# Two-stage attention and top-1 experts: the split of W1 and the first slot's row division moved behind the attention loop, routing moved by three places

## The chip, the cores and the metric

The kernel runs on one core of a Trainium2 chip, as one launch. The metric is the device time of an execution in microseconds. Before the change three executions took 689.18, 688.70 and 688.98 us; their median is 688.98. The profile belongs to a further, profiled execution.

The core has a matrix engine (PE, with its weight loads shown apart as PEld), a vector engine (DVE), a scalar engine (ACT), a general engine (POOL) and a queue engine (SP) that starts DMAs. Each engine runs its own list of instructions in order; semaphores join them.

## The reference

Attention in two steps makes `x`, and a mixture of experts with one expert per row makes the output:

```python
p_packed = sm_attn(p, k, v)              # batch 8, heads 8, p: 32 rows, k and v: 576 rows, head_dim 64
out = sm_attn(q, p_packed, p_packed)     # q: 576 rows
x = out.transpose(0, 2, 1, 3).reshape(4608, 512)

logits = x @ w_gate + modality_bias[modality_id]     # 8 experts
e_idx = argmax(logits); gate_w = softmax(logits)[e_idx]
for e in range(8):                                   # w1: 8 x 512 x 1024, w2: 8 x 1024 x 512
    h = maximum(x[mask_e] @ w1[e], 0)
    out[mask_e] = gate_w[mask_e] * (h @ w2[e])
```

## The kernel before

**Attention.** The work is cut into eight units: unit 2i+g holds the batches 2i and 2i+1 and half g of the heads. A unit goes through: loads of `k`, `v`, `q`; transposes on DVE (`kT`, `qT`, L224); first scores on PE (L234 with `kT`, `pT`); their negated maxima on DVE (`nb`, L246); exponentials on ACT (`a`, L251); transposes of these on PE (L272, L278) with copies on ACT; the packing matmuls (L289); division and sum on DVE (`bd` L294, `pc` L301); a transpose of the packed rows (L308, `ppT` L311); gate products (L321); second scores (L234 with `qT`, `ppT`); their maxima and subtraction on DVE (`m` L336, `mB` L340 and L343); exponentials on ACT (`a2T`, L348); the output matmuls (L357) in three parts; and ACT's copies of each part to `xs` (L364, the unnormalised rows, stored to `x_scr` in HBM) and to `lt` (L366, gate logits and row sums).

**The order.** The units are pipelined. A table written by hand, `ORDER`, names the steps of one period; each has a number of `>` that says how many units ahead it belongs. Inside this loop the order on PE, DVE, ACT and SP is as written; POOL, and everything behind the loop, is ordered by a scheduler. An entry `e` of the table pulls one piece, up to the next `yield`, out of a list `todo`. That list first holds constants and then gets `route(i)` once both units of pair i have finished their output matmuls.

**Routing.** `route(i)` runs `routing(i)` for the 1152 rows of pair i: logits, the arg maximum and a scan on DVE (L400 to L425, ending in `inc`), prefix sums on PE (L431 to L433, which wait for `inc`), places and gate weights (L436 to L452, `dsi` and `meta`), and nine scatters of row numbers by POOL (L455). Pair 0 adds the choice of the first expert. Pair 1 adds: the load of that expert's W1 (L631), table a of the slots, the fetches of the lists and rows of slots 0 and 1 by POOL (`pre`: L647, L650), the split of W1, and the row division of slot 0. Pair 2 adds table b. Pair 3 is routed behind the loop, together with table c.

**The split.** `split_w` makes of a weight a rounded high part on ACT (`w1h`, `w2h`, L642) and the remainder on DVE (`w1l`, `w2l`, L643), each in four parts of 128x1024. `st_n` divides a slot's gathered rows by their sums on DVE (`rx` L664 and L665, `xn` L666), once for each half of 128 rows.

**Slots.** Behind the loop 19 slots of up to 256 rows each follow. A slot: transposes of `xn` (PE L673), high and low part (`x_hl`, ACT L675, DVE L676), W1 products (PE L686: high by high, high by low, low by high), ReLU in two parts (ACT L690, DVE L691), W2 products (PE L723), scaling (ACT L727) and a scatter of output rows by POOL (L728). Rows of the slot after next are gathered meanwhile (L647, L650). Weights are split again, under an `If`, only where the expert changes. The first `If` (L834, in `sw(0, 0)`) is about W1 of the first slot, whose W1 is already split; it isn't taken.

Of the kernel before, what the change touches and what calls it, by code (L numbers as in the profile page):

```python
# [23 lines left out]
def packed_attn_moe_kernel(  # L24
# [75 lines left out]
    def routing_consts(pool):  # L100
        for z in range(0, PAD, P):
            nc.sync.dma_start(lst.rearrange("(e r) w -> r e w", e=E)[z:z + P], pad)
        mid4 = pool.tile([P, NP, NC, 2], I32, name="mid4")
        bias2 = sm.tile([P, 2, E], F32, name="bias2", bufs=1)
        nc.sync.dma_start(bias2, mod_bias[None].broadcast_to([P, 2, E]))
        nc.sync.dma_start(mid4.rearrange("p i c w -> p i (c w)"),
                          mod_id.bitcast(I32).rearrange("(i p m) -> p i m", p=P, m=2 * NC))
        for w in range(2):
            nc.gpsimd.iota(meta.rearrange("p (i c) w -> p i c w", c=NC)[:, :, :, w], pattern=[[P * NC, NP], [1, NC]],
                           base=0, channel_multiplier=NC)  # L110
        nc.gpsimd.tensor_copy(out=m1, in_=mid4[:, :, :, 0])
        m1v = m1.rearrange("p i c -> p (i c)")[:, :, None]
        nc.gpsimd.tensor_scalar(out=m0, in0=m1v, scalar1=-1.0, scalar2=1.0, op0=ALU.mult, op1=ALU.add)
        bias_t = pool.tile([P, NT, E], F32, name="bias_t")
        nc.gpsimd.tensor_tensor(out=bias_all, in0=m0.broadcast_to([P, NT, E]),
                                in1=bias2[:, 0:1, :].broadcast_to([P, NT, E]), op=ALU.mult)
        nc.gpsimd.tensor_tensor(out=bias_t, in0=m1v.broadcast_to([P, NT, E]),
                                in1=bias2[:, 1:2, :].broadcast_to([P, NT, E]), op=ALU.mult)
        nc.gpsimd.tensor_tensor(out=bias_all, in0=bias_all, in1=bias_t, op=ALU.add)
# [11 lines left out]
    xts = [cw.tile([P, 2, 2, GW], F32, name=f"xt{n}") for n in range(2)]  # L131
# [8 lines left out]
    W = dict(raw1=cw.tile([P, KD * F], F32, name="raw1"))  # L140
# [41 lines left out]
    def load_p(q, i0, i1):  # L182
        q.dma_start(pz[:, 4 * i0:4 * i1], p.rearrange("b (g h) j d -> (h j) (b g) d", h=HG)[:, 4 * i0:4 * i1])
# [335 lines left out]
    def first_expert():  # L519
        cnt, mxc = st_("cnt"), st_("mxc", 1)  # L520
        tt(out=cnt, in0=base[1], in1=base0, op=ALU.subtract)
        nc.vector.tensor_reduce(mxc, cnt, axis=AX.X, op=ALU.max)
        nc.vector.scalar_tensor_tensor(out=cnt, in0=cnt, scalar=mxc, in1=desc[:, 0, :], op0=ALU.is_equal, op1=ALU.mult)
        e0 = const.tile([P, 1], F32, name="e0")
        nc.vector.tensor_reduce(e0, cnt, axis=AX.X, op=ALU.max)
        tsc(out=e0, in0=e0, scalar1=-1.0, scalar2=float(E), op0=ALU.mult, op1=ALU.add)
        e0i = const.tile([P, 1], I32, name="e0i")
        nc.vector.tensor_copy(out=e0i, in_=e0)
        return e0, e0i
# [87 lines left out]
    def val(tb, s, col, engines, lo, hi):  # L617
        return nc.values_load(tb[s:s + 1, col:col + 1], engines=engines, min_val=lo, max_val=hi,  # L618
                              skip_runtime_bounds_check_because="bounded by the routing")
# [5 lines left out]
    def load_w(w, which, e):  # L625
        src, n = ((w1, KD), (w2, KF))[which]
        m = src.shape[2]
        d = w["raw" + "12"[which]].rearrange("p (j f) -> p j f", j=n)
        sv = src[ds(e, 1)].rearrange("a (j p) f -> p (a j) f", p=P)
        for j in range(0, n, n // 2):  # L630
            ins = nc.sync.dma_start(d[:, j:j + n // 2], sv[:, j:j + n // 2])  # L631
        return ins_of(ins)

    def split_w(w, which, eng=None, zs=range(4)):
        hi, lo = w["12"[which] + "h"], w["12"[which] + "l"]
        n, m = hi.shape[1], hi.shape[2]
        r = w["raw" + "12"[which]].rearrange("p (j f) -> p j f", j=n)
        for z in zs:
            c = (slice(None), slice(z * n // 4, (z + 1) * n // 4), slice(None))
            if which == 0:  # L640
                c = (slice(None), slice(None), slice(z * m // 4, (z + 1) * m // 4))
            nc.scalar.copy(out=hi[c], in_=r[c])  # L642
            (eng or nc.vector).tensor_tensor(out=lo[c], in0=r[c], in1=hi[c].bitcast(F32), op=ALU.subtract)  # L643
# [16 lines left out]
    def st_n(xt, M):  # L660
        for t in range(2):
            xr = xt[:, t].rearrange("p g (r k) -> p (g r) k", r=4)
            rs = sm.tile([P, H, 1], F32, name="rx")
            nc.vector.tensor_scalar_add(rs, xr[:, :, D:XW], 1e-9)  # L664
            nc.vector.reciprocal(rs, rs)  # L665
            tt(out=M["xn", t].rearrange("p (h d) -> p h d", d=D), in0=xr[:, :, 0:D], in1=rs.broadcast_to([P, H, D]),  # L666
               op=ALU.mult)
# [74 lines left out]
    def pre(n):  # L742
        if n < NS_:
            fetch(*slot_of(n), mts[n % 4], xts[n % 2])

    E0 = []
    with ExitStack() as actx:
        A = dict(ld=actx.enter_context(tc.tile_pool(name="ld", bufs=1)), lp=actx.enter_context(tc.tile_pool(name="lp", bufs=1)),
                 ps=actx.enter_context(tc.tile_pool(name="ps", bufs=4, space=PSUM)))
        us = [attention(n // 2, n % 2, lts[n // 2], A) for n in range(NU)]  # L750

        def rest():
            routing_consts(A["lp"])
            yield

        def route(i):
            yield from routing(i, lts[i], A["ps"])
            if i == 0:
                E0.extend(first_expert())
                yield  # L760
            if i == NA[0] - 1:
                E0.append(val(E0[1], 0, 0, (ET.SP,), 0, E - 1))
                load_w(W, 0, E0[2])
                yield
                T.append((yield from table_phase("a", E0[0], NA[0], None, SA[0])))
                yield
                for n in range(2):
                    pre(n)
                for z in range(4):
                    split_w(W, 0, None, (z,))  # L770
                    yield
                st_n(xts[0], W)
                yield
            if i == NA[1] - 1:
                T.append((yield from table_phase("b", T[0]["last"], NA[1], T[0]["used"], SA[1] - SA[0])))

        todo, seen = [rest()], {}

        def more():
            while todo:  # L780
                try:
                    next(todo[0])
                    return
                except StopIteration:
                    todo.pop(0)

        def step(m, nm):
            next(us[m][nm])
            if m == 0 and nm == "dk":
                load_p(nc.scalar, 0, 2)  # L790
                load_p(nc.scalar, 2, NP)
            if nm == "k0" and m in (0, 1, 2, 3):
                prep_p(A["ps"], 2 * m, nc.scalar.copy if m else nc.vector.tensor_copy)
            seen[m, nm] = seen.get((m, nm), 0) + 1
            if nm[0] == "x" and m % 2 and m // 2 < NA[1] and all(seen.get((m, f"x{z}"), 0) == 3 for z in range(3)):
                todo.append(route(m // 2))

        with tc.manual_schedule(engines={ET.PE, ET.DVE, ET.Activation, ET.SP}):
            for n in range(-6, NU + 6):
                for z in ORDER.split():  # L800
                    nm = z.lstrip("<>")
                    m = n + z.count(">") - z.count("<")
                    if nm == "e":
                        if 0 <= m:
                            more()
                    elif 0 <= m < NU:
                        step(m, nm)
            while todo:
                more()
    wraw = ctx.enter_context(tc.tile_pool(name="wraw", reuse_waits="tile", bufs=1))  # L810
# [147 lines left out]
```

## Time and profile before

| what | value |
|---|---|
| median of three executions | 688.98 us (688.70 to 689.18) |
| the profiled execution | 689.62 us |
| its span, first to last instruction | 688.0 us |
| mean granted clock of PE in the span | 0.935 |
| PE busy | 585.0 us, 85% of the span |
| DVE busy | 296.8 us, 43% |
| ACT busy | 208.1 us, 30% |
| POOL busy | 195.1 us, 28% |

The shares are averages over two stages: some 213 us of attention, in which PE, DVE and ACT wait for each other, and the slots. In the rows below, a line such as `L643 DVE TENSOR_TENSOR w1l<-raw,w1h x3` means three instructions of line 643 on DVE that write `w1l` from `raw` and `w1h`; the bracket names the idle time of the engine ahead of them and what ended it. One execution of the split of W1 (four parts) lies in the loop; three more lie in the slots, at 337, 426 and 653 us.

### The profile page before, as it was taken

What the parts mean: (1) busy time and instruction counts of PE and PEld (TensorE: products, weight loads), DVE (VectorE), ACT (ScalarE), POOL (GpSimd) and SP (SyncE); (2) the same over time, 40 slices, a digit from 0 to 9 for tenths busy, and PEclk for the clock granted to TensorE, in tenths of its full rate; (3) what the DMA queues carried; (4) which work ended last, traced back from release to release, by engine and by line L of the source; (5) the groups of instructions that cost most, each with busy time, mean ns of one, the idle gap of its engine ahead of it and who ended that gap; (6) DMA issues with size and microseconds to landing.
All of it is one profiled execution on the core that took longest, in us unless ns stands there. A gap on an engine that the chain in (4) does not pass through costs nothing. (4 is left out here: it accounts for less than half of the span.)

```text
span 688.0 us, 13217 instructions
## 1 busy us (share of the span) xinstructions
PE 585.0 (85%) x5156; PEld 511.0 (74%) x5156; DVE 296.8 (43%) x701; ACT 208.1 (30%) x373; POOL 195.1 (28%) x226
## 2 busy tenths in 40 slices
PE   2687876765674889999999999899999999999990
PEld 1566654453553879898998898888998899889980
DVE  3375974877785632222451123712311231122290
ACT  1355532424334112121441125411221122122360
POOL 4000113043233633212312343412331233223340
PEclk9999988877776999999999999999999999999996
DMA  9464797770381544111196122631111111112121
GB/s 300 166 229 167 223 337 206 263 280 20 116 316 71 186 156 155 46 46 47 48 335 232 37 66 68 223 108 49 49 50 45 48 48 47 47 49 48 44 61 28
DMA packets 39053, 87.02 MB, mean 126 GB/s; under 512 B 11120, under 2 KB 11120, under 8 KB 37936
## 3 DMA queue, kind: packets, MB, share of 16 engines
q1 hardware_dynamic: 26560, 63.15, 25.9%
q0 software_dynamic: 9264, 22.13, 10.9%
q8 instruction: 52, 0.85, 0.5%
q10 hardware_dynamic: 3136, 0.56, 0.5%
q14 instruction: 41, 0.34, 0.2%
HBM read 66.42 MB, written 19.39 MB: 125 GB/s over the span
## 5 line engine op out<-in xcount | busy, mean ns | idle before, releaser
L686 PE MATMUL ps_h<-x_hl,w1h 128*128 128x256 f32 x1088 | 203.6, 286 | 2.1 <-ACT w1h L642 0.7
L686 PEld LDWEIGHTS ps_h<-x_hl,w1h 128*128 128x128 f32 x1088 | 171.9, 192 | 5.5 <-ACT w1h L642 1.1
L686 PE MATMUL ps_h<-x_hl,w1l 128*128 128x256 f32 x544 | 154.2, 283 | 4.5 <-DVE pref L590 2.4
L691 DVE SCALAR_TENSOR_TENSOR hl<-ps_h,hh 128x512 fp32r<-128x512 f32 x68 | 46.8, 691 | 216.2 <-ACT hh L690 191.7
L723 PE MATMUL ps_o<-w2h,hh 128*128 128x512 f32 x296 | 116.3, 393 | 0.8 <-ACTq L852 0.8
L723 PE MATMUL ps_o<-w2h,hl 128*128 128x512 f32 x296 | 116.1, 392 | 0.0
L723 PE MATMUL ps_o<-w2l,hh 128*128 128x512 f32 x296 | 115.9, 392 | 0.0
L650 POOL DMA_INDIRECT xt<-x_scr,mt x92 | 93.1, 1012 | 71.2 <-issue 24.2
L686 PEld LDWEIGHTS ps_h<-x_hl,w1l 128*128 128x128 f32 x544 | 104.3, 192 | 5.4 <-DVE pref L590 2.6
L690 ACT ACTIVATE hh<-ps_h 128x512 fp32r<-128x512 f32 x68 | 40.6, 599 | 173.8 <-PE ps_h L686 98.5
L728 POOL DMA_INDIRECT out_dram<-ot,mt x37 | 38.6, 1044 | 179.5 <-ACT ot L727 113.0
L727 ACT ACTIVATE ot<-ps_o,mt 128x512 f32<-128x512 f32 x37 | 25.5, 690 | 131.2 <-PE ps_o L723 105.9
L723 PEld LDWEIGHTS ps_o<-w2h,hl 128*128 128x128 f32 x296 | 55.8, 188 | 11.5
L723 PEld LDWEIGHTS ps_o<-w2h,hh 128*128 128x128 f32 x296 | 55.7, 188 | 11.5 <-ACTq L852 1.2
L357 PE MATMUL ps<-bd,a2T 128*128 128x146 f32 x288 | 53.6, 343 | 12.1 <-ACT a L251 5.7
L723 PEld LDWEIGHTS ps_o<-w2l,hh 128*128 128x128 f32 x296 | 55.7, 188 | 10.9
L357 PEld LDWEIGHTS ps<-bd,a2T 128*128 128x128 f32 x288 | 47.3, 232 | 20.9 <-ACT a L251 7.9
L455 POOL DMA_INDIRECT lst<-meta,dsi x36 | 34.9, 970 | 84.7 <-DVE meta L452 33.2
L647 POOL DMA_DIRECT2D mt<-lst x23 | 17.3, 752 | 72.1 <-DMA out_dram<-ot,mt 40.6
L673 PE MATMUL ps_t<-ident,xn 128*128 128x128 f32 x168 | 26.5, 284 | 10.3 <-ACT lt L366 6.1
L289 PE MATMUL ps<-ld_v,a1T 64*64 64x128 f32 x576 | 23.3, 313 | 11.3 <-ACT a1T L280 9.1
L664 DVE TENSOR_SCALAR rx<-xt 128x8 f32<-128x8 f32 x44 | 6.0, 171 | 59.9 <-DMA xt<-x_scr,mt 59.9
(190 smaller groups left out, 671.9 us busy)
## 6 DMA issues: line engine op xcount, KB each, us to landing
raw<-in_moe_w_dram SPq DMA_DIRECT2D x24, 1024.0 KB
x_scr<-xs SPq DMA_DIRECT2D x8, 1170.0 KB
raw<-in_k_dram SPq DMA_DIRECT2D x16, 576.0 KB
ld_v<-in_v_dram SPq DMA_DIRECT2D x16, 576.0 KB
raw<-in_q_dram SPq DMA_DIRECT2D x16, 576.0 KB
xt<-x_scr,mt POOLq DMA_INDIRECT x92
out_dram<-ot,mt POOLq DMA_INDIRECT x37
lst<-meta,dsi POOLq DMA_INDIRECT x36
```

Of the source, the lines that this page charges most:

```text
L289: nc.tensor.matmul(pp[64 * u:64 * u + 64, a, 0:P].rearrange("p (r d) -> p r d", r=2), a1T[rows, c, 64 * u:64 * u + 64], v_t[rows, 2 * u:2 ...
L357: nc.tensor.matmul(xp[:, a, 2 * c * XL:2 * c * XL + 2 * XL], a2T[:, 3 * z + c, a], bd[:, a].rearrange("p r k -> p (r k)"), start=True, sto ...
L455: ins = ins_of(nc.gpsimd.indirect_dma_start(out=lst, out_offset=bass.IndirectOffsetOnAxis(ap=dsi[:, c:c + 1], axis=0), in_=meta[:, i * NC ...
L647: ins = [nc.gpsimd.dma_start(mt, lst[ds(off, P2), :].rearrange("(t p) w -> p t w", p=P))]
L650: ins.append(nc.gpsimd.indirect_dma_start(out=xt[:, t, g], out_offset=None, in_=x_scr[g][0:NA[ph] * 2 * S] if ph < 2 else x_scr[g], in_off ...
L673: nc.tensor.transpose(out=ps[:, j], in_=M["xn", t][:, j * P:j * P + P], identity=ident)
L686: nc.tensor.matmul(ps[:, f], M[a][:, j, (f0 + f) * P:(f0 + f) * P + P], x[:, j, b], start=(m == 0), stop=(m == 3 * KD - 1))
L690: ia = nc.scalar.activation(out=M["hh"][:, fs], in_=ps, func=AF.Relu)
L691: iv = nc.vector.scalar_tensor_tensor(out=M["hl"][:, fs], in0=ps, scalar=0.0, in1=M["hh"][:, fs].bitcast(F32), op0=ALU.max, op1=ALU.subtract)
L723: nc.tensor.matmul(op, M[a][:, j, t * P:t * P + P], M[b][:, j, :], start=(n == 0), stop=(n == 3 * KF - 1))
L727: nc.scalar.activation(out=ot, in_=op, func=AF.Copy, scale=mt.bitcast(F32)[:, t, 2:3])
L728: nc.gpsimd.indirect_dma_start(out=out, out_offset=bass.IndirectOffsetOnAxis(ap=mt[:, t, 1:2], axis=0), in_=ot, in_offset=None, bounds_che ...
```

## The change

Two edits. Three bare `yield`s stand at the start of every `route(i)`: each piece of routing comes three `e` entries later. And the four parts of the split of W1, with the row division of slot 0, leave `route(1)`, where each was pulled by an `e`, and stand behind the loop's last step, ahead of what is left in `todo`.

```diff
         def route(i):
+            yield
+            yield
+            yield
             yield from routing(i, lts[i], A["ps"])
             if i == 0:
                 E0.extend(first_expert())
@@
                 yield
                 for n in range(2):
                     pre(n)
-                for z in range(4):
-                    split_w(W, 0, None, (z,))
-                    yield
-                st_n(xts[0], W)
-                yield
             if i == NA[1] - 1:
@@
                     elif 0 <= m < NU:
                         step(m, nm)
+            for z in range(4):
+                split_w(W, 0, None, (z,))
+            st_n(xts[0], W)
             while todo:
                 more()
```

On DVE, around the first maxima of unit 7 (`nb`) and the second maxima of unit 6 (`m`, `mB`), the list before is:

```order
L541 CAST tab_a<-tab_f 128x7
L643 TENSOR_TENSOR w1l<-raw_111,w1h 128x4x256 x3
L246 TENSOR_REDUCE nb<-ps 128x1 x2
L643 TENSOR_TENSOR w1l<-raw_111,w1h 128x4x256
L664 TENSOR_SCALAR rx<-xt_104 128x8
L665 RECIPROCAL rx<-rx 128x8
L666 TENSOR_TENSOR xn_106<-xt_104,rx 128x512
L664 TENSOR_SCALAR rx<-xt_104 128x8
L665 RECIPROCAL rx<-rx 128x8
L666 TENSOR_TENSOR xn_107<-xt_104,rx 128x512
L336 TENSOR_REDUCE m_1968<-ps 128x9 x2
L340 STREAM_TRANSPOSE mB<-m_1968 128x576
```

At the same place of DVE, the list now is:

```order
L541 CAST tab_a<-tab_f 128x7
L246 TENSOR_REDUCE nb<-ps 128x1 x2
L336 TENSOR_REDUCE m_1952<-ps 128x9 x2
L340 STREAM_TRANSPOSE mB<-m_1952 128x576
L336 TENSOR_REDUCE m_1957<-ps 128x9 x2
L343 TENSOR_TENSOR mB<-ps,mB 128x576
```

The split and the division are gone from between table a and the maxima of both units; ACT's casts of `w1h` are gone from around the exponentials of unit 7 in the same way.

On PE, between unit 7's gate products (L321) and its second scores (L234 with `qT`), the list before is:

```order
L321 MATMUL ps<-wg_132,ppT 32x16 x13
L834 UNCONDITIONAL_BRANCH
L840 UNCONDITIONAL_BRANCH
L321 MATMUL ps<-wg_132,ppT 32x16 x3
L431 LDWEIGHTS ones_b
L431 MATMUL ps<-inc,ones_b 128x72
L432 LDWEIGHTS negtri
L432 MATMUL ps<-oh,negtri 128x72
L433 LDWEIGHTS ones_b
L433 MATMUL ps<-inc,ones_b 128x8
L234 MATMUL ps<-qT,ppT 32x288 x32
```

At the same place of PE, the list now is:

```order
L321 MATMUL ps<-wg_132,ppT 32x16 x16
L234 MATMUL ps<-qT,ppT 32x288 x32
L357 MATMUL ps<-bd_114,a2T_126 128x146 x6
L431 LDWEIGHTS ones_b
L431 MATMUL ps<-inc,ones_b 128x72
L432 LDWEIGHTS negtri
L432 MATMUL ps<-oh,negtri 128x72
L433 LDWEIGHTS ones_b
L433 MATMUL ps<-inc,ones_b 128x8
L357 MATMUL ps<-bd_115,a2T_127 128x146 x18
```

The prefix sums of pair 2 stand behind the second scores and part of unit 6's output now. In the same way those of pairs 0 and 1 moved from ahead of the second scores of units 3 and 5 to behind their transposes; those of pair 3, which stood inside slot 0's W1 products, now stand ahead of slot 0. On DVE the chain L400 to L425 of pair 2 still stands ahead of unit 7's second maxima; the steps from L436 to L445, which stood ahead of them too, now follow them.

On DVE behind the loop, the list now has, after 35 rows of pair 3's routing and table b, two parts of `w2l` among eight short rows, and then:

```order
L541 CAST tab_b<-tab_f 128x7
L643 TENSOR_TENSOR w1l<-raw_111,w1h 128x4x256 x4
L664 TENSOR_SCALAR rx<-xt_104 128x8
L643 TENSOR_TENSOR w2l<-raw_2300,w2h 128x1024 x2
L443 CAST dsi<-dsf 128x9
L475 TENSOR_SCALAR tl_f<-rem 128x8
L497 TENSOR_SCALAR key<-eidx,last_b 128x8
L618 TENSOR_LOAD tab_a
L835 COMPARE_AND_BRANCH
```

Then come the first division of slot 0 (`xn_106`), the second (`xn_107`, nine rows later), and the low parts `x_hl`. So all four parts of `w1l` and of `w2l` now stand ahead of slot 0's rows on DVE; before, `xn` and `w1l` were made in the loop, and the four parts of `w2l` stood behind slot 0's `x_hl`. On ACT the four casts of `w1h`, and then those of `w2h`, stand ahead of slot 0's `x_hl`. On POOL the gathers of slots 2 and 3 stood ahead of pair 3's nine scatters, and stand behind them now. On SP the load of the first W1 stands behind one load of `v` that it preceded.

## The prediction

> **What bounds the kernel now.** I read the slices and the chain of work that ended last first, then the table of windows, then the rows around the holes.
>
> ```profile
> PE   2687876765674889999999999899999999999990
> PE ps_h L686 18%; PE ps_o L723 18%; PE ps_h L706 2%; PE ps_t L673 2%; POOL xt L650 1%; DVE w1l L643 1%; DVE w2l L643 0%; DMA xt<-x_scr,mt 0%; POOL out_dram L728 0%; DVE hs L712 0%; ACT hh L713 0%; ACT hs L711 0%; DVEq L618 0%; DVE x_hl L676 0%; ACT x_hl L675 0%
> ...
> 189.00:206.00 17.00, 11.90 (x140) 9.75 (x139) 13.95 (x61) 6.10 (x13) 4.88 (x6) 0.70 0.86 319
> 206.00:223.00 17.00, 7.13 (x35) 6.03 (x34) 10.03 (x38) 7.78 (x13) 5.89 (x7) 0.69 0.19 72
> 223.00:240.00 17.00, 15.20 (x107) 14.10 (x107) 10.79 (x43) 2.55 (x5) 11.87 (x11) 0.91 0.55 188
> 240.00:257.00 17.00, 14.64 (x78) 12.73 (x77) 6.20 (x35) 2.62 (x5) 6.76 (x7) 0.90 0.44 143
> 257.00:274.00 17.00, 17.00 (x120) 15.68 (x119) 3.46 (x5) 4.24 (x7) 6.12 (x7) 1.00 0.48 165
> ```
>
> A slice is 17.2 us, a window row gives its length and then the busy time of PE, PEld, DVE, ACT and POOL, the granted clock, and DMA. From 257 us PE is busy 17.00 of 17.00 at full clock, and the chain consists of the slots' matmuls. Ahead of that PE has holes: 7.13 busy in 206 to 223, at clock 0.69. The change alters no matmul. Its worth is therefore how much earlier or later PE enters its full stretch **with the same work behind it**. I split that at one event, the last attention copy to `lt`, which ends at 213.38 (the row below that starts at 213.12): what the loop gains ahead of it, and what the slots lose behind it.
>
> The page belongs to an execution of 689.62 us with a span of 688.0; the median of the three runs shown, 688.98, is 0.64 lower. I sum against the span and carry the difference to the median.
>
> **The loop gains: waits of PE on routing.**
>
> ```profile
> 89.44 0.24 PE L431 MATMUL ps<-inc,ones_b 128*128 128x72 bf16 x1 [2.83 <-DVE inc L425]
> 134.03 0.24 PE L431 MATMUL ps<-inc,ones_b 128*128 128x72 bf16 x1 [3.86 <-DVE inc L425]
> 191.55 0.19 PE L431 MATMUL ps<-inc,ones_b 128*128 128x72 bf16 x1 [2.07 <-DVE inc L425]
> ```
>
> Columns: start, duration, what ran, and in brackets the idle time ahead and what ended it. Three times the prefix sums of routing stand in front of a unit's second scores (L234 with `qT`) and PE waits for DVE. Three places later they stand behind those scores, so the first two waits, 2.83 + 3.86 = 6.7 us, have other PE work in front of them. Ends: 6.7 if that work covers them, 0 if DVE, which has the same chain to run, is late with the next maxima instead. I take 6.7, since the rows name nothing else that PE waited for there. The third is treated below.
>
> **The loop gains: the split and the first rows.**
>
> ```profile
> 162.85 3.49 DVE L643 TENSOR_TENSOR w1l<-raw,w1h 128x1024 fp32r<-128x1024 f32 x3
> 166.25 1.42 DVE L246 TENSOR_REDUCE nb<-ps 128x1 f32<-128x576 f32 x2
> 175.34 0.17 DVE L664 TENSOR_SCALAR rx<-xt 128x8 f32<-128x8 f32 x1 [5.15 <-DMA xt<-x_scr,mt]
> 177.44 0.84 DVE L336 TRANSPOSE_TENSOR_REDUCE m<-ps 128x9 f32<-128x288 f32 x2
> ...
> 167.83 1.03 ACT L642 CAST w1h<-raw 128x1024 fp32r<-128x1024 f32 x1
> 168.76 0.74 ACT L251 ACTIVATE a<-ps,nb 128x576 f32<-128x576 f32 x1
> ...
> 167.98 3.29 PE L357 MATMUL ps<-bd,a2T 128*128 128x146 f32 x12 [4.99 <-ACT a L251]
> 181.92 0.85 PE L357 MATMUL ps<-bd,a2T 128*128 128x146 f32 x2 [1.17 <-ACT a2T L348]
> 183.66 2.80 PE L357 MATMUL ps<-bd,a2T 128*128 128x146 f32 x10 [0.88 <-ACT a2T L348]
> ```
>
> For unit 7 the maxima `nb` wait on DVE behind three parts of the split: 3.4 us (166.25 less 162.85), and PE idles 4.99 us for what follows from them. A cast of `w1h` stands between the two exponentials: 0.9 us. The row division waits 5.15 us for the gathered rows, and unit 6's second maxima (L336, at 177.44) are queued behind it; without it they follow `nb` at once, so PE's two later waits for `a2T`, 1.17 + 0.88 = 2.05, go. Together 3.4 + 0.9 + 2.05 = 6.35 us.
>
> **What is late next at unit 7.**
>
> ```profile
> 178.89 1.86 PE L289 MATMUL ps<-ld_v,a1T 64*64 64x128 f32 x26 [0.99 <-issue]
> ...
> 183.92 0.22 DVE L400 TENSOR_SCALAR rs<-lt 128x72 f32<-128x72 f32 x1 [0.80 <-ACT lt L366]
> 185.49 2.63 DVE L224 STREAM_TRANSPOSE qT<-raw 128x1152 f32<-128x1152 f32 x2
> 191.19 0.31 DVE L425 TENSOR_TENSOR_SCAN inc<-cmask,oh 128x72 bf16<-128x72 f32 x1
> 191.84 0.23 DVE L436 TENSOR_TENSOR dst<-ps,run 128x72 f32<-128x72 f32 x1 [0.35 <-PE ps L433]
> 192.78 0.23 DVE L445 TENSOR_TENSOR lg<-lg,mxl 128x72 f32<-128x72 f32 x1
> 194.21 0.85 DVE L336 TRANSPOSE_TENSOR_REDUCE m<-ps 128x9 f32<-128x288 f32 x2 [1.20 <-PE ps L234]
> ```
>
> PE no longer waits 2.07 us in front of unit 7's scores, but DVE's order still holds the chain L400 to L425 ahead of unit 7's maxima. That chain takes 191.50 - 183.92 less the 2.63 of `qT` inside it = 5.0 us; laid behind `qT` without gaps it ends some 10 us after the pack's last matmul (180.75), where the maxima now start 13.5 after. Of those 3.5 the 2.05 above is already counted, and I take 1.1 of the rest.
>
> ```profile
> 209.77 0.96 POOL L455 DMA_INDIRECT lst<-meta,dsi  x1 [0.30 <-issue]
> ...
> 212.41 0.82 ACT L364 COPY xs<-ps 128x780 f32<-128x780 f32 x1 [5.41 <-remote]
> 213.12 0.26 ACT L366 COPY lt<-ps 128x108 f32<-128x108 f32 x1
> ```
>
> The last `xs` copy waits 5.41 us for something "remote" and starts 1.7 us after the last of POOL's nine scatters ends (210.73). These need `meta` (L452), which follows unit 7's maxima. The six steps from L436 to L445, 193.01 - 191.84 = 1.2 us, ran ahead of the maxima and now run behind them, so the scatters start 1.2 us later against the maxima. Ends: 0 or 1.2 lost; I take 1.2, as the copy follows the scatters in the rows.
>
> Loop in all: 6.7 + 6.35 + 1.1 - 1.2 = **13.0 us earlier**, so `lt` ends at about 200.4. Ends: 6.3 without the first term; 16.4 if the scatters cost nothing and PE's 2.27 us of "issue" holes inside the pack (the last, 0.99, is shown), which lie beside the gathers of slot 0, go too.
>
> **What stands behind the loop.**
>
> ```profile
> 213.43 1.97 PE L673 MATMUL ps_t<-ident,xn 128*128 128x128 f32 x8 [6.09 <-ACT lt L366]
> 220.88 0.58 PE L686 MATMUL ps_h<-x_hl,w1h 128*128 128x256 f32 x1
> ...
> 217.63 0.16 DVE L603 TENSOR_TENSOR used_b<-used_b,used_a 128x8 f32<-128x8 f32 x1
> 219.03 0.22 DVE L418 TENSOR_REDUCE mde<-eq 128x9 f32<-128x72 f32 x1
> 220.05 0.78 DVE L676 TENSOR_TENSOR x_hl<-ps_t,x_hl 128x512 fp32r<-128x512 f32 x1
> 221.07 4.62 DVE L643 TENSOR_TENSOR w2l<-raw,w2h 128x1024 fp32r<-128x1024 f32 x4
> ```
>
> Before, PE transposes at once, since `xn` is ready, and the slot flows from 220.88, 7.5 us after `lt`. After, `xn` stands on DVE behind this: the routing chain, 5.0 us, which waits for that `lt`; 24 small steps laid between its own, at (219.03 - 217.63)/11 = 0.127 us a step, 3.0; four parts of `w2l`, 4.62; four parts of `w1l`, as many elements each, 4.62; 15 more small steps, 1.9; a load and branch on DVE, not shown alone, between 0 and 0.85 (the step from L590 to L613 in the rows below), taken 0.7; the first division, 0.7. That is 20.5 us. The second (eight small steps and 0.7) makes 22.2. Four transposes (half of 1.97), their cast and, ahead of `x_hl` (0.78) on DVE, a division of slot 1 with small steps add some 4, so the slot flows about 26.2 us after `lt`: **18.7 later than the 7.5 of before**. ACT's casts (`w1h` 1.03 each, then `w2h`) lie beside the chain; if ACT were late, it would cost what DVE waits. On SP, W1's load moves behind one load of `v`; its split is now some 60 us later, which hides that. W2's load stays ahead of slot 0. On POOL the lists and rows of slot 0 move three places with their routing and are needed only behind `lt`.
>
> ```profile
> 220.90:226.00 5.10, 5.10 (x26) 5.01 (x26) 5.10 (x8) 0.59 (x1) 4.02 (x3) 0.50 0.20 46
> 246.00:251.00 5.00, 5.00 (x28) 4.62 (x27) 2.02 (x7) 1.18 (x2) 1.51 (x3) 0.66 0.82 238
> ...
> 244.70 0.15 DVE L590 TENSOR_TENSOR pref<-tab_f 1x1 f32<-1x1 f32 x1
> 245.55 0.16 DVE L613 TENSOR_TENSOR tab_f<-red,tab_f 128x1 f32<-128x1 f32 x1 [0.70 <-DVE pref L590]
> 233.61 0.47 DVE L664 TENSOR_SCALAR rx<-xt 128x8 f32<-128x8 f32 x2 [5.80 <-DMA xt<-x_scr,mt]
> ```
>
> Some of that comes back, since W2's split and the routing are then done. Before, PE loses behind 220.88: 1.8 and 2.36 us idle (the windows from 223 and 240) and, at half clock, 2.55 (half of 5.1) and 1.7 (0.34 of 5.0): 8.4. After, it starts at half clock again (2.55), and `rx` of slot 2 waits for rows whose gathers POOL now has behind the last scatters; I take a third of the 5.80 that DVE stood there, 1.9. That saves 8.4 - 4.45 = 4.0, with ends 0 and 5.9. Behind the loop: 18.7 - 4.0 = **14.7 later**, with ends 12.8 and 18.7.
>
> The page "TensorE: Matmul & The Clock Gate" of the Trainium skill, Part 1, says that the clock rises after about 3.4 us of sustained work. Here it stayed at 0.50 for 5.1 us of full work, which the trace decides; by the page the term of 2.55 would be an estimated 1.7 and the sum 0.85 lower.
>
> **Sum.** +14.7 - 13.0 = +1.7 us: span 689.7, execution 691.3, median 690.7.
>
> **The rivals.**
> *The loop gains more than the slots lose (faster).* The place is the end of `lt`: ahead of 213.4 - 14.7 = 198.7 the change wins. For it: PE's holes in the pack beside the gathers, and DVE's 13.95 of 17.00 busy from 189, which the split no longer adds to ahead of unit 7. At the ends it is 16.4 gained against 12.8 lost, -3.6: median 685.4. Against it: the scatters still end just ahead of `lt`.
> *The waits on routing come back (far slower).* DVE runs the same chain, and maxima are behind it where PE was. Then only 6.3 to 8 is gained ahead of `lt`, and +6.7 to +8.4 gives 695.7 to 697.4. The last scatters also fall beside slot 0's first transposes; a delay like the 5.41 "remote" there adds up to 5.
> *Nothing measurable.* Loop and slots cancel, if the chain on DVE is some 2 us shorter than I laid it: 687.6 to 690.4. Were the matmuls themselves the limit ahead of 257 us, the change would also do nothing; the 7.13 of 17.00 speaks against that.
>
> **Chances.** The forecast has 0.42 (688 to 693.5 alone), the faster rival 0.27, the far slower one 0.21, cancelling 0.10. A measurement of this kernel tells about 0.2% from no change: 1.4 us, the band from 687.6 to 690.4. Of the forecast's 0.42, 0.10 lies inside that band, 0.02 below and 0.30 above. Faster 0.27 + 0.02 = 0.29, same 0.10 + 0.10 = 0.20, slower 0.30 + 0.21 = 0.51. The range takes in most of both outer rivals: 684.5 to 698.5.
>
> **What would show it.** Right: no idle time of PE ahead of L431 at units 3, 5 and 7; `nb` directly behind `tab_a`; `lt` ending near 200; PE idle some 20 us behind it, with `w1l` and `w2l` one after the other on DVE; L686 flowing some 26 us after `lt`. Wrong: `lt` ahead of 198.7 or behind 206, L686 within 20 us of `lt`, or a new wait in front of unit 7's maxima longer than the chain of 5.0.

## The result, and the profile after

The changed kernel takes 697.73 us (median of four executions, 697.12 to 698.02) against 689.08 us for the kernel before in the same comparison: 1.0117 times as long, interval 1.0092 to 1.0142. The profiled execution takes 697.12 us with a span of 695.5, which is 7.5 more than the 688.0 of before.

The page of the kernel after, the slices (17.4 us each) and the granted clock, and then its table of windows (length; PE, PEld, DVE, ACT, POOL busy; clock; DMA):

```profile
PE   2687869657731799999999999899999999999990
PEclk9999996976865789999999999999999999999996
...
172.00:189.00 17.00, 13.64 (x158) 9.93 (x154) 8.15 (x18) 3.64 (x10) 5.11 (x6) 0.80 0.47 146
189.00:206.00 17.00, 7.15 (x39) 6.47 (x39) 12.08 (x54) 8.31 (x15) 7.36 (x8) 0.77 0.39 149
206.00:223.00 17.00, 1.07 (x7) 0.91 (x7) 16.80 (x65) 6.36 (x8) 4.42 (x6) 0.50 0.21 59
223.00:240.00 17.00, 14.01 (x87) 12.23 (x85) 8.55 (x47) 2.35 (x4) 13.04 (x14) 0.80 0.95 275
240.00:257.00 17.00, 13.87 (x70) 12.07 (x71) 7.27 (x16) 4.05 (x7) 2.68 (x4) 0.72 0.36 118
```

From 206 to 223 us PE now does 1.07 us of work while DVE is busy for 16.80 of 17: the stretch that the prediction laid behind the loop is there. What wasn't expected stands further down: 223 to 257 is no fuller than before (14.01 and 13.87 against 15.20 and 14.64), although the splits are done by then.

PE after, from the timeline (start, duration, what ran, idle time ahead and what ended it):

```profile
130.62 1.75 PE L234 MATMUL ps<-qT,ppT 32*32 32x288 f32 x61
156.33 1.80 PE L234 MATMUL ps<-kT,pT 32*32 32x288 f32 x29 [5.72 <-issue]
160.34 2.36 PE L234 MATMUL ps<-kT,pT 32*32 32x288 f32 x16 [0.72 <-issue]
177.35 0.42 PE L289 MATMUL ps<-ld_v,a1T 64*64 64x128 f32 x2 [0.98 <-issue]
189.11 0.21 PE L431 MATMUL ps<-inc,ones_b 128*128 128x72 bf16 x1 [0.24 <-DVE inc L425]
222.22 1.08 PE L673 MATMUL ps_t<-ident,xn 128*128 128x128 f32 x4 [11.88 <-DVE rx L664]
225.92 1.36 PE L686 MATMUL ps_h<-x_hl,w1h 128*128 128x256 f32 x3
236.95 0.40 PE L686 MATMUL ps_h<-x_hl,w1h 128*128 128x256 f32 x2 [0.71 <-issue]
240.52 0.56 PE L686 MATMUL ps_h<-x_hl,w1l 128*128 128x256 f32 x1 [1.05 <-issue]
245.46 0.60 PE L686 MATMUL ps_h<-x_hl,w1h 128*128 128x256 f32 x2 [0.83 <-issue]
```

The wait ahead of L431 is gone where it was looked for (0.24 us at unit 7; the second scores of unit 5 run on at once). At units 3 and 5 PE still stands 1.56 us ahead of it, now for `mB`. But unit 7's first scores, which took from 157.8 to 160.9 us before, now start at 149.9 and end at 163.2: PE stands there for "issue", waiting for nothing that the profile shows. Call such idle time a hole. PE has more of them in the pack and in slot 0, in steps of about 0.7 us.

The longest hole is in truth ACT's. PE's remaining first scores stand behind ACT's copy of the gate products, `bd` (L325), and ACT starts it late, after an idle time that the profile can only call "remote"; PE goes on 0.24 us behind it. Before the change it was ACT's `ppT` (L311), for which unit 6's gate products waited. First the row of before, then that of after:

```profile
156.25 0.38 ACT L311 ACTIVATE ppT<-ps 128x256 f32<-128x256 f32 x1 [9.90 <-remote]
...
156.09 0.19 ACT L325 COPY bd<-ps 128x32 f32<-128x32 f32 x1 [6.71 <-remote]
```

POOL after, at the same times:

```profile
148.98 0.96 POOL L455 DMA_INDIRECT lst<-meta,dsi  x1 [33.83 <-DVE meta L452]
159.07 0.96 POOL L455 DMA_INDIRECT lst<-meta,dsi  x1 [0.30 <-issue]
221.08 1.02 POOL L455 DMA_INDIRECT lst<-meta,dsi  x1 [4.20 <-DVEq L835]
242.18 0.95 POOL L650 DMA_INDIRECT xt<-x_scr,mt  x1 [0.30 <-issue]
```

The nine scatters of pair 1 run from 148.98 to 160.0; behind the loop nine scatters and eight gathers run without a break from 221.08 to 243.1. The holes on PE lie inside these bursts and end 0.1 to 2.3 us behind them. The view of waits sums PE's idle time by what ended it (us in total, times, longest). Before:

```profile
PE ps L321 <- issue: 8.7, 9, 4.7
PE ps L289 <- issue: 2.3, 4, 1.0
PE ps L357 <- issue: 1.1, 1, 1.1
```

And after:

```profile
PE ps L234 <- issue: 7.7, 5, 5.7
PE ps_h L686 <- issue: 3.6, 5, 1.1
PE ps L289 <- issue: 2.9, 7, 1.0
PE ps_o L723 <- issue: 1.7, 2, 0.8
PE ps L357 <- issue: 1.5, 2, 1.3
```

So there were 12.1 us of such holes before and 17.4 after, in the same stretches of POOL's work but under other work of PE: before, pair 1's burst fell on unit 6's gate products (5.3 of the 8.7 us at L321), after, on unit 7's first scores (7.2 of the 7.7 at L234); the rest of these two rows lies beside pair 0's burst.

DVE and ACT after, at the places of the sum:

```profile
163.19 1.42 DVE L246 TENSOR_REDUCE nb<-ps 128x1 f32<-128x576 f32 x2 [1.20 <-PE ps L234]
213.74 4.62 DVE L643 TENSOR_TENSOR w1l<-raw,w1h 128x1024 fp32r<-128x1024 f32 x4
218.35 2.36 DVE L643 TENSOR_TENSOR w2l<-raw,w2h 128x1024 fp32r<-128x1024 f32 x2
221.38 0.69 DVE L666 TENSOR_TENSOR xn<-xt,rx 128x512 f32<-128x512 f32 x1
...
203.59 0.81 ACT L364 COPY xs<-ps 128x780 f32<-128x780 f32 x1 [2.90 <-remote]
204.30 0.26 ACT L366 COPY lt<-ps 128x108 f32<-128x108 f32 x1
```

`nb` of unit 7 no longer waits for a split; it waits for PE, and comes 3.1 us earlier than before instead of ten. The last `lt` ends at 204.56, 8.8 us earlier. `xn` is done at 222.1, PE transposes it from 222.22, having waited 11.88 us, and the slot flows from 225.92, 21.4 us behind `lt`, where it was 7.5.

### The profile page after: what moved, and what is told of

Read it like the earlier page. It is cut to its first block, busy times and chain, and to the rows that moved or that the text cites. A ratio compares the mean times of both kernels' runs of the same rounds, so it can differ in the third digit from the quotient of the medians.

```text
span 695.5 us, 13226 instructions
## 1 busy us (share of the span) xinstructions
PE 588.6 (85%) x5156; PEld 510.8 (73%) x5156; DVE 296.3 (43%) x701; ACT 208.3 (30%) x373; POOL 193.1 (28%) x226
## 5 line engine op out<-in xcount | busy, mean ns | idle before, releaser
L686 PE MATMUL ps_h<-x_hl,w1h 128*128 128x256 f32 x1088 | 202.9, 285 | 3.2 <-issue 2.5
L686 PEld LDWEIGHTS ps_h<-x_hl,w1h 128*128 128x128 f32 x1088 | 171.9, 192 | 6.3 <-issue 2.9
L686 PE MATMUL ps_h<-x_hl,w1l 128*128 128x256 f32 x544 | 154.4, 284 | 3.3 <-DVE w1l L643 2.2
L691 DVE SCALAR_TENSOR_TENSOR hl<-ps_h,hh 128x512 fp32r<-128x512 f32 x68 | 46.7, 691 | 224.1 <-ACT hh L690 189.2
L723 PE MATMUL ps_o<-w2h,hh 128*128 128x512 f32 x296 | 116.3, 393 | 1.0 <-ACTq L853 0.8
L650 POOL DMA_INDIRECT xt<-x_scr,mt x92 | 90.4, 982 | 73.2 <-issue 24.8
L686 PEld LDWEIGHTS ps_h<-x_hl,w1l 128*128 128x128 f32 x544 | 104.3, 192 | 5.2 <-issue 2.4
L357 PE MATMUL ps<-bd,a2T 128*128 128x146 f32 x288 | 49.8, 326 | 10.9 <-ACT a2T L348 4.8
L357 PEld LDWEIGHTS ps<-bd,a2T 128*128 128x128 f32 x288 | 44.0, 218 | 18.6 <-ACT a L251 8.5
L234 PE MATMUL ps<-kT,pT 32*32 32x288 f32 x512 | 29.2, 525 | 13.8 <-issue 7.7
L289 PE MATMUL ps<-ld_v,a1T 64*64 64x128 f32 x576 | 26.9, 342 | 11.5 <-ACT a1T L280 7.8
## 6 DMA issues: line engine op xcount, KB each, us to landing
raw<-in_moe_w_dram SPq DMA_DIRECT2D x24, 1024.0 KB, 10.6
```

The source lines that it names most:

```text
L234: nc.tensor.matmul(t[u][32 * h:32 * h + 32, hf, :HS].rearrange("p (c q) -> p c q", c=NC), l[qd, db, 32 * h:32 * h + 32], r[qd, h, :, db, : ...
L289: nc.tensor.matmul(pp[64 * u:64 * u + 64, a, 0:P].rearrange("p (r d) -> p r d", r=2), a1T[rows, c, 64 * u:64 * u + 64], v_t[rows, 2 * u:2 ...
L357: nc.tensor.matmul(xp[:, a, 2 * c * XL:2 * c * XL + 2 * XL], a2T[:, 3 * z + c, a], bd[:, a].rearrange("p r k -> p (r k)"), start=True, sto ...
L650: ins.append(nc.gpsimd.indirect_dma_start(out=xt[:, t, g], out_offset=None, in_=x_scr[g][0:NA[ph] * 2 * S] if ph < 2 else x_scr[g], in_off ...
L686: nc.tensor.matmul(ps[:, f], M[a][:, j, (f0 + f) * P:(f0 + f) * P + P], x[:, j, b], start=(m == 0), stop=(m == 3 * KD - 1))
L691: iv = nc.vector.scalar_tensor_tensor(out=M["hl"][:, fs], in0=ps, scalar=0.0, in1=M["hh"][:, fs].bitcast(F32), op0=ALU.max, op1=ALU.subtract)
```

## The experiments

**Theory A**: the loss lies in DVE's order behind the loop, the loop's gain is real. **Theory B**: indirect DMAs that POOL issues back to back hold up the other engines' instructions, and the change loses by moving these bursts onto other work. The experiments fell on three chips: the first eight on one, the next three on a second, the last on a third. The kernel before takes 687 to 688 us on the first and the last of these and 666.8 on the second. Ratios are each to the kernel before on the same chip. On the first chip single executions of the kernel before spread from 682 to 699 us, hence the wide intervals.

### One part of the change at a time

**The three places alone.**

```diff
         def route(i):
+            yield
+            yield
+            yield
             yield from routing(i, lts[i], A["ps"])
```

> The three places alone; split of W1 and the row division stay in the loop. Theory A (the loss sits behind the loop, in DVE's order; the loop's gain is real): the waits ahead of L431 go, lt ends 4 to 7 us before the 213.4 of before, the slot flows some 7.5 us behind it, and the time is 682 to 686 us. Theory B (POOL's bursts of indirect DMAs stall whichever engine work lies beside them; later routing only moves the burst onto other work): lt ends within 2 us of 213.4 and the time is 687 to 691 us, with 'issue' holes on PE inside unit 7's scores or pack, beside the scatters or gathers.

Measured: 692.61 us, 1.0056 (1.0016 to 1.0096): slower without any split behind the loop. `lt` ends at 207.6, so the loop does gain, and slot 0 flows by 217. Then it is lost. Its waits:

```profile
PE ps L234 <- issue: 13.2, 5, 10.6
PE ps_o L723 <- issue: 6.6, 1, 6.6
PE ps_h L686 <- issue: 4.0, 3, 1.8
```

Unit 7's scores have a hole of 10.6 us beside pair 1's scatters (150.3 to 161.3). Behind the loop, scatters and gathers run as one burst here too, from 226.9 to 248.8, and PE has a hole of 6.6 us and more inside it. Theory A falls for the time of this half of the change, though it had `lt` right (4 to 7 us earlier; it came 5.8 earlier, where B allowed 2). B had the holes in unit 7's scores right, and too small a loss.

**The split and the division alone.**

```diff
-                for z in range(4):
-                    split_w(W, 0, None, (z,))
-                    yield
-                st_n(xts[0], W)
-                yield
...
+            for z in range(4):
+                split_w(W, 0, None, (z,))
+            st_n(xts[0], W)
             while todo:
```

> The split of W1 and the row division behind the loop, routing at its old places. Theory A: the loss behind the loop stays whole (slot 0 flows 21 to 22 us behind lt, not 7.5), the loop gains what stood ahead of unit 7's maxima, 4 to 6 us, and the waits ahead of L431 (2.8, 3.9) are back: 696 to 701 us. Theory B says the same of the slots, but lt no later than with both edits (204.6), so 695 to 698 us.

Measured: 701.85 us, 1.0150 (1.0061 to 1.0239); `lt` ends at 207.96. Theory A had `lt` right (4 to 6 us earlier) and missed the time by 0.9 us; B missed both. By the ratios the halves cost 0.56% and 1.50% alone and 1.17% together. The sum of the two, 2.06%, has an interval of about 1% either way, so whether they add is not shown.

**Both, with the division left in the loop.**

```diff
                 for n in range(2):
                     pre(n)
+                st_n(xts[0], W)
+                yield
...
-            st_n(xts[0], W)
             while todo:
```

> Both edits, but the row division of slot 0 stays in the loop, so that only the split of W1 stands behind it. Theory A: xn is ready at lt, PE transposes at once, x_hl is made ahead of the splits on DVE, and only the w1l parts are late; PE waits for w1l some 15 us behind lt, and the division's wait for the gathered rows is back ahead of unit 6's maxima: 690 to 695 us. Theory B: the same slots, but unit 6 pays the wait for the gathers (5 us or more): 694 to 699 us.

Measured: 713.63 us, 1.0331 (1.0224 to 1.0438). Both numbers missed. Part of the reason is in one row of PE:

```profile
230.74 0.58 PE L686 MATMUL ps_h<-x_hl,w1l 128*128 128x256 f32 x1 [9.95 <-DVEq L836]
```

With `xn` ready, the list for DVE has `w1l` behind all of `w2l` and table b, so that slot 0 waits for it until 230.7, 24 us behind `lt`. So the slot flows even later than in the changed kernel (225.92). That is 4.8 of the 17.7 us by which this trace is longer than the changed kernel's (spans 713.2 and 695.5). Up to 260 us PE then loses some 7 us more, idle or at half clock (20.14 busy of 29.26 us at clock 0.66, against 28.69 of 34.08 at 0.81), and at 415.7 it stands 5.53 us for "DVEq". Why these two came with the edit was not looked into.

**Both, with the split left in the loop.**

```diff
                 for n in range(2):
                     pre(n)
+                for z in range(4):
+                    split_w(W, 0, None, (z,))
+                    yield
...
-            for z in range(4):
-                split_w(W, 0, None, (z,))
             st_n(xts[0], W)
```

> Both edits, but the split of W1 stays in the loop (three places later), so that only the row division stands behind it. Theory A: w2l stands ahead of xn on DVE, so the slot flows 15 to 18 us behind lt; the loop is as with both edits or 1 to 3 us longer: 692 to 696 us. Theory B: the same within a us, since neither the scatters nor the gathers move against the change.

Measured: 695.87 us, 1.0109 (1.0014 to 1.0205), and the slot flows 16.7 us behind `lt` (219.28 against 202.58). Both theories allow it; it doesn't tell them apart.

### The bursts themselves

**Pair 1's scatters held apart, in the changed kernel.**

```diff
         for c in range(NC):
+            of = dsi[:, c:c + 1]
+            if i in (1,):
+                dsp = sm.tile([P, 64], I32, name="dsp", bufs=1)
+                nc.gpsimd.tensor_copy(out=dsp, in_=of.broadcast_to([P, 64]))
+                of = dsp[:, 0:1]
             ins = ins_of(nc.gpsimd.indirect_dma_start(
-                out=lst, out_offset=bass.IndirectOffsetOnAxis(ap=dsi[:, c:c + 1], axis=0),
+                out=lst, out_offset=bass.IndirectOffsetOnAxis(ap=of, axis=0),
```

> The changed kernel; each of pair 1's nine scatters takes its places from a small copy that POOL makes, with one buffer, so that a scatter waits for the end of the one before and the nine no longer run back to back. Theory A (the loss is DVE's order behind the loop): no effect on lt (204.6), 697 to 699 us. Theory B (indirect DMAs issued back to back by POOL hold up the instruction supply of the other engines): the hole of 5.7 us and more in PE's first scores of unit 7 goes, lt ends 4 to 7 us earlier, 691 to 694 us, unless the gathers of slots 0 and 1, now later, hold up the pack or the scores behind.

Measured: 696.75 us, 1.0150 (1.0074 to 1.0225). The time says nothing, the trace a great deal:

```profile
150.57 1.39 PE L234 MATMUL ps<-kT,pT 32*32 32x288 f32 x49 [0.73 <-ACT bd L325]
243.39 0.80 PE L691 MATMUL ps_h<-x_hl,w1h 128*128 128x256 f32 x2 [18.12 <-DVE hl L696]
...
190.65 0.26 ACT L366 COPY lt<-ps 128x108 f32<-128x108 f32 x1
```

The hole in unit 7's scores is gone (149.1 to 152.1 us), and PE's short wait there is put down to ACT's `bd` by name. `lt` ends at 190.9, 13.7 us ahead of the changed kernel, twice what theory B expected. More than one burst moved: the gathers of slot 0 and pair 2's scatters came later too, and with them went the 2.9 us of holes in the pack and the 2.9 us of "remote" ahead of the last copy. Then PE waits 18.12 us for `hl` (L691 here is L686 with the lines shifted): the held-up scatters push all of POOL's later work back, and the gathers for slot 2, on whose row division DVE's list waits ahead of a further `hl`, run at 238 to 248 us, behind pair 3's scatters. The gain is real and is given back to POOL's queue.

**Nine more scatters, in the changed kernel.** They go to a second list that nothing reads.

```diff
             scattered[i].append(ins)
+        if i == 1:
+            for c in range(NC):
+                ins = ins_of(nc.gpsimd.indirect_dma_start(
+                    out=lst2, out_offset=bass.IndirectOffsetOnAxis(ap=dsi[:, c:c + 1], axis=0),
+                    in_=meta[:, i * NC + c, :], in_offset=None))
+                tc.declare_no_dep(ins, group="scat2", reason="every row of the list is written once")
+                tc.add_to_no_dep_group("scat2", ins)
```

> The changed kernel with nine more scatters right behind pair 1's, to a second list that nothing reads: POOL's burst there is 18 long instead of 9. No other engine waits for them, and slot 0's gathers, which come behind, have 40 us of room. Theory A: no effect, 697 to 699 us. Theory B: PE's hole ends some 11 us later, behind the 18th, and lt and the time are 5 to 11 us later: 703 to 709 us.

Measured: 716.45 us, 1.0418 (1.0340 to 1.0497), `lt` at 222.9: 18 us behind the changed kernel on both counts, more than B expected. POOL's burst lasts from 153.1 to 175.5 here, and PE (L235 is L234):

```profile
163.35 1.80 PE L235 MATMUL ps<-kT,pT 32*32 32x288 f32 x28 [8.66 <-issue]
178.63 0.93 PE L235 MATMUL ps<-kT,pT 32*32 32x288 f32 x13 [1.47 <-issue]
...
PE ps L235 <- issue: 21.3, 13, 8.7
```

No engine waits for these scatters, and the idle time in unit 7's scores grows from 7.2 to 18.3 us, until some three us behind the last of them (the other 3 of the 21.3 us lie beside pair 0's burst). Theory A can't give this.

**Pair 0's scatters held apart, in the kernel before** (the same edit with `i in (0,)`).

> The kernel before, with pair 0's nine scatters held apart by the copy. Nothing reads that list until pair 1 is routed. Theory A: 687 to 689.5 us, no difference. Theory B: the stretch of unit 4 around 103 to 116 us (its transposed packed rows, then first scores) loses its holes and all behind it moves up by 3 to 6 us: 682 to 686 us.

Measured: 691.48 us, 1.0070 (1.0028 to 1.0112): slower, against theory B's number. Unit 4's first scores do lose their hole (106.7 to 109.2 us; they ended at 116.3 before). But POOL ends pair 0's scatters only at 156.1, starts pair 1's at 156.4 instead of 144.9, and the rows of slot 0 land later. DVE still waits for them in the loop ahead of unit 6's maxima, 20.05 us (5.15 before), and PE behind it:

```profile
180.26 0.17 DVE L669 TENSOR_SCALAR rx<-xt 128x8 f32<-128x8 f32 x1 [20.05 <-DMA xt<-x_scr,mt]
...
186.84 0.85 PE L357 MATMUL ps<-bd,a2T 128*128 128x146 f32 x2 [16.21 <-ACT a2T L348]
```

**The three places alone, with pair 3's scatters held apart** (the same edit with `i in (3,)`).

> The three places alone, with pair 3's nine scatters held apart; in POOL's order the gathers of slots 2 and 3 now come ahead of them, and there is no burst of 17 indirect DMAs any more. Theory A: as with the three places alone (692.6) within a few us. Theory B: PE loses 4 to 7 us between 220 and 255 us instead of 13.7, and the time is 682 to 687 us, below the kernel before.

Measured: 684.74 us, 0.9966 (0.9929 to 1.0003), 7.9 us less than the three places alone, as B expected: the long burst of 17 is gone and with it the hole of 6.6 us. The interval just takes in no change, so this is not shown to be faster than the kernel before.

### Another chip, and the change once more

These three came back with the kernel before at 666.81 us.

> The changed kernel with pair 3's scatters held apart, as in the run of the three places alone with the same edit; the gathers of slots 2 and 3 now mix with them. The loop and the order on DVE stay as changed. Theory A: 697 to 699 us. Theory B: PE's holes between 236 and 246 us shrink from the 9.4 us lost there to some 5, 692 to 695 us. Both: lt near 204.6 and the slot's flow some 21.5 us behind it.

> The changed kernel with the scatters of pairs 1 and 3 held apart. Theory B: lt ends near 191 as with pair 1's alone (the run that gave 696.8 us lost the gain again in one wait of 18 us for the rows of slot 2, whose gathers came behind pair 3's scatters at 226 to 248); with these held apart the gathers come first, the wait shrinks to 8 to 12 us, and the time is 686 to 691 us. Theory A has no lever here: 697 to 699 us.

> The kernel before with pair 3's scatters held apart; the gathers of slots 2 and 3 stand ahead of them already, so only the burst of nine at 236 to 247 us is broken up. Theory B: PE's hole of 2.4 us there and the half clock behind it go, 2 to 4 us less than before: 684 to 687 us, no slower than the three places with the same edit (684.7). Theory A: no difference.

Measured: the changed kernel with pair 3's scatters apart 673.89 us, 1.0105 (1.0060 to 1.0151); with those of pairs 1 and 3 apart 688.46, 1.0335 (1.0294 to 1.0376); the kernel before with pair 3's apart 672.27, 1.0098 (1.0063 to 1.0134). All numbers missed, also as differences to the kernel before (7.1, 21.7 and 5.5 us more), and this chip has hardly any of the holes. Waits of PE for "issue", first in the changed kernel with pair 3's scatters apart:

```profile
PE ps L234 <- issue: 1.3, 2, 0.9
PE ps L357 <- issue: 1.2, 1, 1.2
```

And in the kernel before with the same edit:

```profile
PE ps L357 <- issue: 1.0, 1, 1.0
```

The scatters of pair 1 still run back to back in both (136.4 to 147.4 us in the first of them), yet unit 7's first scores beside them take 137.2 to 139.3. So a burst alone doesn't make a hole; what else it takes is not known. Where there is none, holding scatters apart cost time: POOL's output scatters queue behind the copies, and PE waits 3.85 us for ACT's `ot` at 244 us in the kernel before with this edit.

The two also compare the loops without holes. Their last `lt`:

```profile
181.03 0.26 ACT L366 COPY lt<-ps 128x108 f32<-128x108 f32 x1
```

```profile
194.35 0.26 ACT L366 COPY lt<-ps 128x108 f32<-128x108 f32 x1
```

The changed loop ends 13.3 us earlier here, and slot 0 flows 21.4 us behind `lt` (202.71) against 7.1 (201.72), so 14.3 later. By the medians the changed kernel is 1.6 us slower. Only two kernels with held-apart scatters are compared in this, and their executions spread over eight to ten us; by the two ratios the difference is 0.5 us, with an interval of some 4 us either way. So the size of the change's cost on this chip is not shown.

**The changed kernel once more**, no edit.

> The changed kernel once more, unaltered, on whichever chip comes. The two chips so far differ: on one, PE has long 'issue' holes beside POOL's bursts (before 688), on the other hardly any (before 666.8). Theory B says that the loss of the change hangs on them: if its trace shows holes of 5 us and more in unit 7's first scores, lt ends near 204 and the change costs 7 to 11 us; if it shows none, lt ends near 181, 13 us ahead of the 194.6 of the kernel with the old loop there, and the change costs 0 to 4 us. Theory A: 7 to 11 us on either.

Measured: 695.73 us against 686.98, 1.0135 (1.0106 to 1.0164), on a chip with holes. Its row in unit 7's scores:

```profile
155.28 1.84 PE L234 MATMUL ps<-kT,pT 32*32 32x288 f32 x29 [7.28 <-ACT bd L325]
158.56 1.70 PE L234 MATMUL ps<-kT,pT 32*32 32x288 f32 x16 [1.44 <-issue]
```

Pair 1's scatters run there from 146.5. `lt` ends at 201.1 and the cost is 8.8 us, within the 7 to 11 that both theories gave for a chip with holes. The first hole is put down to ACT's `bd` by name here. As in every other run with this hole, PE goes on 0.24 us behind the start of that copy. The changed kernel without edits was not seen on the chip without holes; whether it costs less there stays open.

## Why the prediction was right, and where it was wrong

The sign was right and the time lies inside the range (684.5 to 698.5), near its upper end; it does so because the range took in most of the far slower rival. The likeliest time, 690.7, was 7.0 us short. The steps follow; the first needs these rows of PE after, from units 3 to 5:

```profile
93.27 0.21 PE L431 MATMUL ps<-inc,ones_b 128*128 128x72 bf16 x1 [1.56 <-DVE mB L343]
94.94 0.30 PE L278 MATMUL ps<-ident,a 128*128 128x128 f32 x1 [1.42 <-DVE mB L343]
134.91 1.76 PE L357 MATMUL ps<-bd,a2T 128*128 128x146 f32 x12 [2.54 <-ACT a L251]
```

- **Waits on routing go (6.7).** The step failed. The waits for `inc` went, but PE now waits for what DVE makes behind the same chain (the rows above). From 76 us to unit 6's gate products PE waited 6.7 us for `inc`, 0.8 for `mB` and 0.3 for `a` before; after, 6.2 for `mB` and 3.8 for `a`. PE is free for these gate products 2.3 us earlier (149.67 against 151.97), not 6.7. On the chip without holes it is 2.4 (136.98 against 139.38), so this doesn't need the bursts. The prediction had named this end, DVE late with the next maxima, and took the other "since the rows name nothing else that PE waited for there". Unit 7's first scores then start 7.9 us earlier than before, where they had stood behind the burst, and end 2.2 later, as the burst now lies beside them; the 8.7 us of "issue" at L321 in the view of waits of before had named such a loss.
- **Split and division out of the loop (6.35).** Right as a mechanism: `nb` follows table a, unit 6's maxima follow `nb`, the two waits for `a2T` are gone. Unit 6's second maxima end 12.0 us earlier (170.17 against 182.19). But `nb` waits for the held-up scores, and at unit 7's gate products 4.3 us are left of all gains so far (184.85 against 189.13). On the chip without holes it is 13.4 (161.94 against 175.36). There this stretch gives 11.0, more than the term: its kernel with the old loop waits 6.7 us for `a2T`, not 2.05, and 5.58 us for DVE ahead of unit 6's second scores.
- **Unit 7's order (1.1) and scatters 1.2 later.** From unit 7's gate products to the last `lt` another 4.5 us were gained, where the two terms give -0.1. The wait ahead of L431 is 0.24 instead of 2.07, and the "remote" wait of the last copy fell from 5.41 to 2.90 us instead of holding. The scatters came later by the maxima, as forecast, but by 2.2 us (3.1 behind the last `mB` instead of 0.9).
- **Loop in all.** 13.0 forecast, 8.8 measured.
- **Behind the loop.** The order came as laid out, `w1l` and `w2l` whole ahead of `xn`, but 18.7 was too much: 13.9 measured. DVE fits the small steps of table b between the routing's more closely (from 204.59 to 210.70, 6.1 us, where 8.0 was laid), and the slot starts on the first `x_hl` before the second is complete.
- **What comes back (4.0).** The step failed with its sign. By windows from the flow to 260 us, PE lost 4.16 us idle and 4.3 at half clock before (34.96 busy of 39.12, clock 0.89); after, 5.39 and 6.5 (28.69 of 34.08, clock 0.81): 3.4 more instead of 4.0 less. The wait for slot 2's rows was seen, the burst of 17 indirect DMAs and its holes were not.

-8.8 + 13.9 + 3.4 = +8.5, against 7.5 in the span; the difference of 1.0 is not accounted for. So the change is slower because slot 0 starts 13.9 us later behind `lt` and the loop's gain doesn't reach that.

The chip without holes comes close to the forecast's +1.7, and that is luck. Its loop gained 13.3 us, as 2.4 + 11.0 - 0.1 where the prediction has 6.7 + 6.35 - 0.1. Behind the loop it lost 14.3 where the prediction has 18.7 less 4.0. Errors of four us and more cancel in both.

Of the rivals, the far slower one has the time (695.7 to 697.4, against 697.7) and in part the reason: the waits on routing came back as waits for DVE's maxima and what follows from them, and it gave 6.3 to 8 us ahead of `lt`, where 8.8 came. It had little of the rest: 14.7 later behind the loop was again 18.7 less 4.0, and only its last clause, that the last scatters fall beside slot 0's start, touches the holes. The faster rival needed `lt` ahead of 198.7; the run with pair 1's scatters apart had it at 190.9 and still wasn't faster, because that run moved the loss to POOL's queue.

## What to carry to other kernels

Idle time of an engine that the profile puts down to "issue" or "remote" belongs in the sum of a reordering as a load of its own, with its place: look what POOL issues beside it, and ask on which work the burst falls once its producer moves. When an engine's list holds a chain ahead of work that others need, taking one reader of that chain out of the way doesn't free the next one: here the waits for `inc` became waits for `mB` and `a`. When work moves out of a pipelined stage, look whether the first item that the next stage needs ends up behind it; here all eight parts of two splits stood ahead of one row division. And a gain in the loop is worth what the slowest queue behind it lets through: with the loop 13.7 us shorter, but POOL made late by the held-apart scatters, the wait for its gathers took all of it back.

## What the runs showed of the hardware

- Where the kernel before takes 687 to 689 us, the other engines stood while POOL issued indirect DMAs back to back (one each 1.26 us). In the changed kernel ACT stood 6.71 us ("remote") beside pair 1's nine, and PE, which waited for it, 7.2 us in all; with 18 in a row PE stood 18.3 us, and with the nine held apart this hole was gone. The holes end 0.1 to 3.1 us behind the last DMA of a burst.
- What holds the engines up is not shown. Late refills of instructions would be one cause. The Trainium skill, "Runtime: NRT & Kernel Launch", section "Instruction fetch mechanics", says that instructions stream in by DMA in blocks of 16 KiB and that crossing a block is mostly hidden; the profile's instruction queue with its 52 packets and 0.85 MB has that size. The traces have these packets, though not which engine they are for. In the changed kernel's hole one starts at 155.0 us and takes 1.1 us, just ahead of ACT's copy at 156.09; in the run with nine more scatters one starts at 159.25, also for 1.1 us, and ACT's copy comes only at 163.11. So they don't settle it.
- The holes differ between the chips. Where the kernel before takes 687 to 689 us, its variants without held-apart or added scatters show 12.1 to 25.7 us of "issue" idle time on PE; where it takes 667, the two with pair 3's alone held apart show 1.0 and 2.5. These sums leave out part of the loss: beside pair 0's burst, unit 4's first scores take from 103.0 to 114.0 us in the changed kernel, with 0.5 us of "issue", and from 103.0 to 105.1 on the second chip. Why the chips differ stays open.
